# Seven block products for the first feed-forward product, and a first batch that stays in SBUF

## The chip, the cores and the metric

The program runs on one core of one Trainium2 chip. The metric is the device time of one execution in microseconds (us). The kernel before took 2764.47 us as the median of three runs (2764.15 to 2766.35). Engines are named as in the profile: PE is the matrix engine (PEld its weight loads), DVE the vector engine, ACT the scalar engine, POOL the general-purpose engine, SP the engine that issues most DMAs. The order of the instructions on each engine is fixed when the program is built.

## The reference, cut to what matters

Eight batches of 3008 tokens with 256 channels go through a Fourier mixing layer (FFT over the tokens, a complex 256x256 product, soft threshold, inverse FFT) and then through a feed-forward layer with 2048 hidden units, whose nonlinearity is h*cos(h). Behind the mixing layer `x` has shape (24064, 256), `w_in` (256, 2048) and `w_out` (2048, 256):

```python
def _moe_ref(x, w_in, w_out) -> np.ndarray:
    h = x @ w_in
    g = h * np.cos(h)
    return (g @ w_out).astype(np.float32)
```

The two weights of the feed-forward layer arrive as float64 and are decoded on the chip from their bits.

## The kernel before, in words

Three stages run for each batch `b`. Stage A (`stage_a`) multiplies the tokens by a 64-point Fourier matrix `f1`, stage B (`stage_b`) does the 47-point transforms, the complex product with the Fourier weights (`wmix`), the threshold and the first half of the inverse transform (`inverse`), in four quarters of eight frequencies each; stage C (`stage_c`) does the other half of the inverse for one tile of 512 tokens and leaves the layer's input, channels on the partitions, in SBUF. Between the stages the data goes through scratch tensors in DRAM (`scr1`, `scr2`). A batch has `NTT` = 6 tiles, the last with 448 tokens.

The feed-forward layer then runs for a tile over the `NFC` = 16 blocks of 128 hidden units, one `moe_step` each. Each operand is split into a high and a low part (type fp32r), and three products stand for one: high by high, high by low and low by high. So a step has 6 matmuls of 512 columns for `x @ w_in` (256 channels are two halves `c` of 128; lines 611 to 613) and 6 for the product with `w_out` (two halves `e` of the output channels; lines 593, 594 and 597, in `second`). Between them stand, for the step's 128x512 values in PSUM: the rounding of h/(2 pi) to an integer (ACT, line 618), the remainder (DVE, 619), the sine (ACT, 621), the product with h (DVE, 622), the high part `gh` (ACT, 623) and the low part `gl`, which takes turns between POOL (line 240, `rest_pool`) and DVE (243, `rest`). `second` runs `SKEW` = 3 steps behind, so that these six have the time of three steps; `u` has four buffers and PSUM holds three `ph`, three banks `f` for the Fourier stages, and two `po`.

The Fourier stages of the next batches are generators; `pull` takes a piece of them twice in each step, so that their matmuls stand between those of the feed-forward layer. This work is called **filler** below. Each yields its cost in PE time, and `share` spreads the sum over the tiles. A scheduler of the framework then fixes the order of the instructions on each engine.

The first batch has nobody to stand beside. Its stage A (`stage_a0`, line 299) writes to `scr1` in DRAM (line 302), its stage B loads it back (`load0`, line 360) and takes its 47-point matrices from DRAM through POOL's queue (line 386). In the same stretch the first half of the feed-forward weights is loaded and decoded in pieces of 512 elements per partition (`split_f64`, lines 201 to 212); the second half is decoded in the first tile, 0.62 pieces per step (`W_RATE`).

Of the kernel before, what the change touches and what calls it, by code (L numbers as in the profile page):

```python
# [58 lines left out]
def _constants():  # L59
# [14 lines left out]
    ei = ei.reshape(4, 32, 128).transpose(1, 0, 2).reshape(128, 128) * (2.0 / N)  # L74
# [28 lines left out]
    i1 = i1.reshape(2, 96, 96).transpose(1, 0, 2)  # L103
# [11 lines left out]
def tile_body(ctx: ExitStack, tc, x, w_r, w_i, b_r, b_i, w_in, w_out,  # L115
# [11 lines left out]
    ff = cp.tile([128, 256], F32, name="ff")  # L127
    nc.gpsimd.dma_start(ff, c_ff)
# [12 lines left out]
    def load_constants():  # L141
        with nc.allow_non_contiguous_dma(reason="bias"):
            for r, bsrc in enumerate((b_r, b_i)):
                nc.gpsimd.dma_start(bb[:, r, :], bsrc.rearrange("(c p) -> p c", p=128))
        nc.gpsimd.dma_start(sig, c_sig)
        nc.gpsimd.dma_start(fi[0], c_if)

# [11 lines left out]
    win = cp.tile([128, 2, 2, FF], F32R, name="win")  # L159
    wout = cp.tile([128, 2, NFC, 256], F32R, name="wout")  # L160
# [5 lines left out]
    fi, ws = {}, {}  # L166
# [16 lines left out]
    def load_f64(src):  # L183
        if "pro" in pool:
            raw = pool["pro"].tile([128, 1024], U32, tag="xp", name="raw", bufs=XP_BUFS)
        else:
            raw = wk.tile([128, 1024], U32, tag="raw", name="raw", bufs=1)
        with tc.issue_after(mark["b0"].ins):
            nc.gpsimd.dma_start(raw if len(src.shape) == 2 else raw.rearrange("p (f e) -> p f e", f=2), src)
        return raw  # L190

    def split_f64(hi, lo, raw):
# [3 lines left out]
        m = wk.tile([128, 512], F32, tag="yh", name="wm", bufs=2)  # L196
        a = wk.tile([128, 512], F32, tag="wa", name="wa", bufs=1)
        q = wk.tile([128, 512], F32, tag="yl", name="wq", bufs=2)
# [11 lines left out]
        nc.scalar.copy(hi, a)  # L210
        rest_pool(a, a, hi)
        ve.tensor_tensor(out=lo, in0=a, in1=q, op=ALU.add)  # L212

    pieces = []
    for q in range(4):
        for c in range(2):
            cs = slice(512 * q, 512 * q + 512)
            pieces.append((win[:, 0, c, cs], win[:, 1, c, cs], w_in[128 * c:128 * c + 128, 1024 * q:1024 * q + 1024]))
        for f in (4 * q, 4 * q + 2):
            pieces.append((wout[:, 0, f:f + 2].rearrange("p f e -> p (f e)"),  # L220
                           wout[:, 1, f:f + 2].rearrange("p f e -> p (f e)"),
                           w_out[128 * f:128 * f + 256, :].rearrange("(f p) e -> p f e", p=128)))
    raws, mark = [], {}

    def load_piece():
        k = len(raws)
        if k < len(pieces):
            raws.append(load_f64(pieces[k][2]))

    def moe_w():  # L230
        for k, (hi, lo, _) in enumerate(pieces):
            while len(raws) <= k:
                load_piece()
            split_f64(hi, lo, raws[k])
# [14 lines left out]
    def fps(name):  # L249
        if "pro" in pool:  # L250
            if not banks:
                banks.extend(("f", "h", "o0", "f", "h", "o1", "f", "h"))
            tag = banks.pop(0)
            return ps.tile([128, 512], F32, tag=tag, name=name, bufs=1 if tag[0] == "o" else 3)
        return ps.tile([128, 512], F32, tag="f", name=name, bufs=3)
# [31 lines left out]

    def stage_a0():

        scr1[0] = dr.tile([32, 96, 256], F32, tag="scr1", name="scr1_0")  # L290
        dst = scr1[0].rearrange("s (r i) d -> (s r) i d", r=4)
        xs = []
        for c in range(6):
            xs.append(pool["pro"].tile([128, 1024], F32, tag="xp", name="x0", bufs=XP_BUFS))
            nc.sync.dma_start(xs[c], x[0, :, 1024 * c:1024 * (c + 1)])
        landed("x0", xs[5][:, :1])
        for c in range(12):
            p = fps("pa")
            mm(p, ff[:, :128], xs[c // 2][:, 512 * (c % 2):512 * (c % 2) + 512], start=True, stop=True)
            ao = stage_in("ao0") if c % 2 else stage_out("ao0")  # L300
            mark["a0", c % 2] = (nc.vector.tensor_copy if c % 2 else nc.scalar.copy)(ao, p)
            mark["a0"] = nc.sync.dma_start(dst[:, 2 * c:2 * c + 2, :], ao.rearrange("p (i d) -> p i d", i=2))
            if c == 5:
                load_fourier_w()

    def stage_a(b):
# [4 lines left out]
        def load(c):  # L311
            if c < 12:
                ld[c] = stage_in("xt")
                with tc.issue_after(mark["at0", 2].ins) if b == 1 else ExitStack():
                    nc.sync.dma_start(ld[c], x[b, :, 512 * c:512 * (c + 1)])

        def prep(c):
            if b > 1 and c < 12:
                xt = ld.pop(c)
                xh = wk.tile([128, 512], F32R, tag="xh", name="xh", bufs=3)  # L320
                xl = wk.tile([128, 512], F32R, tag="xl", name="xl", bufs=3)
# [10 lines left out]
        for c in range(12):  # L332
            load(c + ahead)
            prep(c + 1)
            p = fps("pa")
            if b == 1:
                mm(p, ff[:, :128], ld.pop(c), start=True, stop=True)
# [7 lines left out]
            nc.sync.dma_start(dst[:, 2 * c:2 * c + 2, :], ao.rearrange("p (i d) -> p i d", i=2))  # L345
            yield 0.65


    def stage_b(b):
        scr2[b] = dr.tile([4, 24, 32, 256], F32, tag="scr2", name=f"scr2_{b}")  # L350
        dst = scr2[b].rearrange("r i s d -> (r i) s d")
# [4 lines left out]
        def load0(v):  # L356
            if v < 8:
                at0[v] = pool["pro"].tile([128, 1024], F32, tag="xp", name="at0", bufs=XP_BUFS)[:96]
                at0[v] = at0[v].rearrange("p (s d) -> p s d", s=4)
# [401 lines left out]
```

## Time and profile before

The table is of the profiled execution, which took 2764.63 us; 2762.9 of them lie between the first and the last instruction (the span).

| what | us |
|---|---|
| median of three runs | 2764.47 |
| profiled execution, whole | 2764.63 |
| its span | 2762.9 |
| first matmul of the feed-forward layer | 142.5 |
| first output of tile 0 copied from PSUM | 214.9 |
| last output written, issue | 2757.7 |

The last three rows are times from the span's start. A profile gives for each engine the time in which it was busy. A group of instructions shows its line in the kernel, its operation, output and inputs, the shape, the count, the busy time and the mean time of one, and the idle time ahead with what ended it. The chain of waits follows the work that ended last back to its start. There a matmul's length is the distance to the next one, while in a group its length includes the time until its result is out; only the former adds up.

### The profile page before, as it was taken

How to read it: one execution, taken by the hardware profiler on the slowest of the kernel's cores; microseconds unless marked ns; L12 is line 12 of the kernel's file. 1: busy time of each engine (PE TensorE's matmuls, PEld its weight loads, DVE VectorE, ACT ScalarE, POOL GpSimd, SP SyncE). 2: the span in 40 equal slices, each digit the busy share in tenths (PEclk: the TensorE clock that was granted, in tenths of full speed). 3: DMA queues.
4: the chain of work that ended last, by engine and by line, in shares of the span. 5: the costliest groups of instructions: out<-in, count | busy, mean ns of one | idle time of the engine just before them, and what ended most of it. 6: DMA issues, size and time to landing. Idle time of an engine off the chain costs nothing.

```text
span 2762.9 us, 37050 instructions
## 1 busy us (share of the span) xinstructions
PE 2717.8 (98%) x13286; PEld 2298.8 (83%) x13286; DVE 1851.6 (67%) x2920; ACT 1751.5 (63%) x3236; POOL 905.2 (33%) x707
## 2 busy tenths in 40 slices
PE   6899999999999999999999999999999999999999
PEld 4478888888888888888888888888888888888888
DVE  3697766767756776677766777667776677666665
ACT  2566666666666666666666666666666666666666
POOL 3364332334323442243322433233332323222222
PEclk8999999999999999999999999999999999999999
DMA  8421221122111221112211122111222111011000
GB/s 251 156 88 50 78 66 62 47 67 82 44 59 55 68 77 51 53 53 72 71 64 41 58 69 72 64 37 55 70 68 67 31 43 56 28 48 33 8 16 15
DMA packets 115753, 172.34 MB, mean 62 GB/s; under 512 B 13008, under 2 KB 64960, under 8 KB 115568
## 3 DMA queue, kind: packets, MB, share of 16 engines
q1 hardware_dynamic: 109632, 151.04, 17.4%
q0 software_dynamic: 5936, 18.92, 2.2%
q8 instruction: 105, 1.72, 0.3%
q14 instruction: 80, 0.66, 0.1%
HBM read 94.94 MB, written 74.97 MB: 61 GB/s over the span
## 4 chain that ended last, share of the span: by engine, by line
PE 95%; DVE 2%; DMA 2%; ACT 1%; issue 0%; POOL 0%; SPq 0%; ACTq 0%; POOLq 0%; DVEq 0%
PE po L593 12%; PE ph L611 12%; PE po L594 12%; PE po L597 12%; PE ph L613 12%; PE ph L612 12%; PE pb L397 3%; PE pc L574 3%; PE pi L509 3%; PE pw L443 2%; PE pw L441 2%; PE pw L442 2%; PE pt L476 2%; PE pw L437 1%; PE pa L341 1%; PE pa L340 1%
## 5 line engine op out<-in xcount | busy, mean ns | idle before, releaser
L240 POOL TENSOR_TENSOR gl<-u,gh 128x512 fp32r<-128x512 f32 (+1 forms) x384 | 492.3, 1282 | 1536.5 <-ACT gh L623 1254.3
L622 DVE TENSOR_TENSOR u<-ph,u 128x512 f32<-128x512 f32 (+1 forms) x768 | 521.2, 679 | 300.8 <-ACT u L621 287.9
L619 DVE SCALAR_TENSOR_TENSOR u<-ph,u 128x512 f32<-128x512 f32 (+1 forms) x768 | 519.7, 677 | 297.1 <-ACT u L618 295.2
L621 ACT ACTIVATE u<-u 128x512 f32<-128x512 f32 (+1 forms) x768 | 480.0, 625 | 327.8 <-DVE u L619 325.2
L618 ACT ACTIVATE u<-ph 128x512 int32<-128x512 f32 (+1 forms) x768 | 450.8, 588 | 307.2 <-PE ph L613 298.4
L611 PE MATMUL ph<-xTh,win 128*128 128x512 f32 (+1 forms) x1536 | 611.2, 398 | 2.9 <-DVE u L622 2.8
L593 PE MATMUL po<-gh,wout 128*128 128x512 f32 (+1 forms) x1536 | 601.9, 392 | 0.0
L613 PE MATMUL ph<-xTh,win 128*128 128x512 f32 (+1 forms) x1536 | 595.5, 388 | 2.5 <-DVE win L212 2.5
L623 ACT CAST gh<-u 128x512 fp32r<-128x512 f32 (+1 forms) x768 | 468.1, 609 | 204.2 <-DVE u L622 200.6
L594 PE MATMUL po<-gh,wout 128*128 128x512 f32 (+1 forms) x1536 | 595.4, 388 | 0.0
L612 PE MATMUL ph<-xTl,win 128*128 128x512 f32 (+1 forms) x1536 | 594.1, 387 | 0.0
L597 PE MATMUL po<-gl,wout 128*128 128x512 f32 (+1 forms) x1536 | 477.0, 388 | 0.5 <-POOL gl L240 0.5
L243 DVE TENSOR_TENSOR gl<-u,gh 128x512 fp32r<-128x512 f32 (+1 forms) x384 | 316.3, 824 | 79.4 <-ACT gh L623 74.1
L613 PEld LDWEIGHTS ph<-xTh,win 128*128 128x128 f32 x1536 | 288.4, 188 | 57.5 <-DVE win L212 3.0
L611 PEld LDWEIGHTS ph<-xTh,win 128*128 128x128 f32 x1536 | 289.3, 188 | 51.2 <-DVE u L622 3.9
L597 PEld LDWEIGHTS po<-gl,wout 128*128 128x128 f32 x1536 | 286.3, 188 | 54.4 <-POOL gl L240 0.7
L593 PEld LDWEIGHTS po<-gh,wout 128*128 128x128 f32 x1536 | 289.0, 188 | 50.7
L594 PEld LDWEIGHTS po<-gh,wout 128*128 128x128 f32 x1536 | 288.9, 188 | 50.9 <-DVE wout L212 0.4
L612 PEld LDWEIGHTS ph<-xTl,win 128*128 128x128 f32 x1536 | 289.3, 188 | 47.0
L397 PEld LDWEIGHTS pb<-f,at 96*128 96x128 f32 x896 | 121.1, 191 | 9.5 <-DVE Xl L402 0.5
L495 DVE SCALAR_TENSOR_TENSOR yl<-pt,sig,yh 96x256 fp32r<-96x256 f32 x224 | 103.8, 474 | 34.8 <-ACT yh L494 33.4
L240 POOL TENSOR_TENSOR xl<-xt,xh 128x512 fp32r<-128x512 f32 x72 | 99.2, 1378 | 80.1 <-PE pa L342 49.3
(109 smaller groups left out, 2769.7 us busy)
## 6 DMA issues: line engine op xcount, KB each, us to landing
scr<-ao SPq DMA_DIRECT2D x96, 256.0 KB, 2.3
scr<-bo SPq DMA_DIRECT2D x128, 192.0 KB, 2.1
bt<-scr SPq DMA_DIRECT2D x192, 128.0 KB, 2.6
xt<-in_dram SPq DMA_DIRECT2D x84, 256.0 KB, 2.9
at<-scr SPq DMA_DIRECT2D x112, 192.0 KB, 2.6
out_dram<-ob SPq DMA_DIRECT2D x80, 256.0 KB, 2.2
raw<-in_dram POOLq DMA_DIRECT2D x16, 512.0 KB, 4.7
f<-in_dram POOLq DMA_DIRECT2D x56, 144.0 KB, 3.0
```

The costliest lines, as they stand in the source:

```text
L240: return nc.gpsimd.tensor_tensor(out=lo, in0=x, in1=hi.bitcast(F32), op=ALU.subtract)
L593: mm(po[e][:, :n], wout[:, 0, f, es], gh[:, :n], start=f == 0, stop=False)
L594: mm(po[e][:, :n], wout[:, 1, f, es], gh[:, :n], start=False, stop=False)
L597: mm(po[e][:, :n], wout[:, 0, f, es], gl[:, :n], start=False, stop=f == NFC - 1)
L611: mm(h, win[:, 0, c, fs], th[:, c, :n], start=c == 0, stop=False)
L612: mm(h, win[:, 0, c, fs], tl[:, c, :n], start=False, stop=False)
L613: mm(h, win[:, 1, c, fs], th[:, c, :n], start=False, stop=c == 1)
L618: nc.scalar.activation(k[:, :n], h, AF.Identity, bias=0.25, scale=1.0 / TWO_PI)
L619: nc.vector.scalar_tensor_tensor(out=u[:, :n], in0=h, scalar=1.0 / TWO_PI, in1=k[:, :n], op0=ALU.mult, op1=ALU.subtract)
L621: nc.scalar.activation(u[:, :n], u[:, :n], AF.Sin, bias=HALF_PI, scale=TWO_PI)
L622: nc.vector.tensor_tensor(out=u[:, :n], in0=h, in1=u[:, :n], op=ALU.mult)
L623: nc.scalar.copy(gh[:, :n], u[:, :n])
```

## The change: what it does

**Seven products for eight.** Two blocks of hidden units (a pair `fp`) and the two halves of a tile (256 tokens each) are taken together. With the two channel halves this is a product of 2x2 blocks, done by Strassen's scheme in Winograd's form: seven products of 128x128 by 128x256 where there were eight. Each product still has three matmuls, now of 256 columns: 21 per pair, where two steps had 12 of 512. The last tile is also done with 512 columns in this product (before: 448).

- The block sums of the weights are made once, while the weights are decoded (`win_blocks`: four sums on POOL for each quarter of `w_in`; `win` holds seven blocks per pair). The sums of the input are made in `stage_c` for each tile: seven blocks `xh`, `xl`, through four DVE subtractions and one on POOL of 256 columns, and their high and low parts.
- The sums of the results are made in PSUM. `moe_pair` keeps two banks: `hA` with blocks c11 and c22, `hB` with c12 and c21. ACT copies the first product from `hA` to `hB` (line 680) and another to `t5` in SBUF (682); DVE adds `t5` twice (692 and 697, 256 columns each); PE goes on accumulating on what they wrote.
- The nonlinearity is done on the two banks (lines 703, 704, 714, 719 to 721, 726, 728). The low part of `hA` is now always DVE's (line 727, through 267), that of `hB` always POOL's (729, through 264). Half of this work is put off into the next pair (`tail`). `u` has two buffers (`UB`), PSUM two banks each of `hA`, `hB` and `f`.

**The first batch.** Its stage A takes `x` as the stationary operand and the Fourier matrix as the moving one (line 335): 48 matmuls of 128 columns. The result `a0`, channels on the partitions, stays in SBUF. `turn` transposes it, four blocks at a time, on PE (line 397) to what stage B needs. The write to `scr1` and the loads from it are gone for this batch, and the 47-point matrices come early, on SP's queue (`load_f0`).

**Weights.** All of `w_in` (8 pieces) is decoded ahead of the feed-forward layer, and all of `w_out`, in 16 pieces of 256 elements, in the first tile, 2.5 pieces per pair.

**Smaller edits.** `scr2` has another order of axes, so that stage C loads a half tile with one DMA of 256 KB and not two of 128. `wmix` copies two of its three products by ACT into their place, where it copied one. The sums of the two parts in stage B are made in halves of 384 elements on POOL, with one buffer. `xh`, `xl` of stage A have one buffer each.

What the scheduler makes of a pair is seen on PE in the last batch, where no filler stands between. Before, one step stands as the 6 matmuls of `second` and the 6 of the first product (the last three rows stand twice):

```order
L593 MATMUL po_23717<-gh,wout 128x512 [waits Activation_49]
L594 MATMUL po_23717<-gh,wout 128x512
L593 MATMUL po_23718<-gh,wout 128x512
L594 MATMUL po_23718<-gh,wout 128x512
L597 MATMUL po_23717<-gl,wout 128x512 [waits Pool_49]
L597 MATMUL po_23718<-gl,wout 128x512
L611 MATMUL ph<-xTh,win 128x512 [waits DVE_49]
L612 MATMUL ph<-xTl,win 128x512
L613 MATMUL ph<-xTh,win 128x512
```

Now, the same engine and batch. These rows stand behind the first two products of a pair (6 matmuls into `hA`), and ahead of the `gl` matmuls and another whole `second`, behind which come 6 more into `hB`:

```order
L648 MATMUL po_29191<-gh,wout 128x512 [waits Activation_49]
L649 MATMUL po_29191<-gh,wout 128x512
L648 MATMUL po_29192<-gh,wout 128x512
L649 MATMUL po_29192<-gh,wout 128x512
L675 MATMUL hB<-xTh,win 128x256 [waits DVE_49]
L675 MATMUL hB<-xTl,win 128x256
L675 MATMUL hB<-xTh,win 128x256
L675 MATMUL hB<-xTh,win 128x256 [waits Activation_49]
L675 MATMUL hB<-xTl,win 128x256
L675 MATMUL hB<-xTh,win 128x256
L675 MATMUL hA<-xTh,win 128x256 [waits Activation_49]
```

The first three rows into `hB` are the last product of one pair and wait for DVE's second add; the next three belong to the next pair and wait for ACT's copy of line 680. The scheduler has put the first products of a pair ahead of the last of the pair before.

ACT had three instructions per step, here two steps in the last batch:

```order
L618 ACTIVATE u<-ph 128x512 [waits PE_49,Activation_49]
L623 CAST gh<-u 128x512 [waits DVE_49]
L621 ACTIVATE u<-u 128x512 [waits DVE_49]
L618 ACTIVATE u<-ph 128x512 [waits PE_49,Pool_49]
L623 CAST gh<-u 128x512 [waits DVE_49]
```

Now it has eight per pair; the two copies are new, and the second rounding waits for POOL, which must have read the buffer of `u` that it overwrites:

```order
L680 COPY hB<-hA 128x256 [waits PE_49]
L703 ACTIVATE u<-hA 128x512 [waits DVE_49,Activation_49]
L682 COPY t_29929<-hA 128x256
L703 ACTIVATE u<-hB 128x512 [waits PE_49,Pool_49]
L714 ACTIVATE u<-u 128x512 [waits DVE_49]
L719 ACTIVATE u<-u 128x512 [waits DVE_49]
L726 CAST gh<-u 128x2x256 [waits DVE_49]
L728 CAST gh<-u 128x512 [waits DVE_49]
```

And DVE's row of one pair, which had five instructions for two steps (two remainders, two products, one low part) and has seven:

```order
L697 TENSOR_TENSOR hA<-hB,t_29929 128x256 [waits PE_49]
L704 SCALAR_TENSOR_TENSOR u<-hA,u 128x512 [waits Activation_49]
L692 TENSOR_TENSOR hB<-hB,t_29985 128x256 [waits PE_49,Activation_49]
L704 SCALAR_TENSOR_TENSOR u<-hB,u 128x512 [waits Activation_49]
L720 TENSOR_TENSOR u<-hA,u 128x512 [waits Activation_49]
L721 TENSOR_TENSOR u<-hB,u 128x512 [waits Activation_49]
L267 TENSOR_TENSOR gl<-u,gh 128x2x256 [waits Activation_49]
```

The rows show that the two adds (697 of one pair, 692 of the next) stand around the first remainder, so that each waits in line with the nonlinearity.

The diff, cut to what is spoken of:

```diff
-SKEW = 3
-EARLY_W = 8
+EARLY_W = 12
-W_RATE = 0.62
-POOL_GL = (0, 2)
+W_RATE = 2.5
+UB = 2
...
+    def win_blocks(q, w):
+        sm = pool["pro"].tile([128, 1024], F32, tag="xp", name="sm", bufs=XP_BUFS).rearrange("p (r k e) -> p r k e", r=2, k=4)
+        w0, w1 = (a.rearrange("p (r f e) -> p r f e", r=2, f=2) for a in w)
+        po = nc.gpsimd.tensor_tensor
+        po(out=sm[:, :, 0], in0=w0[:, :, 1], in1=w1[:, :, 1], op=ALU.add)
+        po(out=sm[:, :, 1], in0=sm[:, :, 0], in1=w0[:, :, 0], op=ALU.subtract)
+        po(out=sm[:, :, 2], in0=w0[:, :, 0], in1=w0[:, :, 1], op=ALU.subtract)
+        po(out=sm[:, :, 3], in0=w1[:, :, 0], in1=sm[:, :, 1], op=ALU.subtract)
+        for lo, hi, src in ((0, 1, w0[:, :, :1]), (1, 3, w1), (3, 7, sm)):
+            wh, wl = (win[:, h, 2 * q:2 * q + 2, lo:hi] for h in range(2))
+            nc.scalar.copy(wh, src)
+            rest(wl, src, wh)
...
-            mm(p, ff[:, :128], xs[c // 2][:, 512 * (c % 2):512 * (c % 2) + 512], start=True, stop=True)
-            mark["a0"] = nc.sync.dma_start(dst[:, 2 * c:2 * c + 2, :], ao.rearrange("p (i d) -> p i d", i=2))
+            for c in range(2):
+                for i in range(2):
+                    o, k = 256 * c + 128 * i, 512 * (n % 2) + 256 * i + 128 * c
+                    mm(p[:, o:o + 128], xs[n // 2][:, k:k + 128], fi[1], start=o == 0, stop=o == 384,
+                       skip_group_check=True)
...
+        def turn(u):
+            if b == 0 and u < 16:
+                p = fps("pq")
+                for j in range(2):
+                    for c in range(2):
+                        o = 256 * j + 128 * c
+                        nc.tensor.transpose(p[:96, o:o + 128], a0[0][:, c, 2 * u + j], ident)
+                at0[u] = pool["pro"].tile([128, 512], F32, tag="at0", name="at0", bufs=3)[:96]
+                (nc.vector.tensor_copy if u % 2 else nc.scalar.copy)(at0[u], p[:96])
...
-    def moe_step(b, t, f, pull):
+    def moe_pair(b, t, fp, pull):
+        xs = xT[b, t]
+        pa = ps.tile([128, 512], F32, tag="hA", name="hA", bufs=2)
+        pb = ps.tile([128, 512], F32, tag="hB", name="hB", bufs=2)
+        c11, c22, c12, c21 = pa[:, :256], pa[:, 256:], pb[:, :256], pb[:, 256:]
+        def product(dst, wb, xb, first=False, last=False):
+            for n, (h, x) in enumerate(((0, 0), (0, 1), (1, 0))):
+                mm(dst, win[:, h, fp, wb], xs[x][:, xb], start=first and n == 0, stop=last and n == 2,
+                   skip_group_check=True)
+        product(c11, 0, 0, first=True)
+        product(c22, 3, 3, last=True)
+        nc.scalar.copy(c21, c11)
+        t5 = pool["mo"].tile([128, 256], F32, tag="t5", name="t5", bufs=1)
+        nc.scalar.copy(t5, c22)
+        if tail:
+            next(tail[0])
+        old = second(*pend.pop(0)) if len(pend) > 2 else iter(())
+        next(old, None)
+        pull()
+        if tail:
+            next(tail.pop(0), None)
+        product(c11, 1, 1, last=True)
+        product(c21, 4, 5)
+        nc.vector.tensor_tensor(out=c12, in0=c21, in1=t5, op=ALU.add)
+        pull()
+        next(old, None)
+        product(c21, 5, 4, last=True)
+        product(c12, 6, 2, last=True)
+        nc.vector.tensor_tensor(out=c22, in0=c21, in1=t5, op=ALU.add)
...
+        start(pa)
+        pull()
+        if len(pend) > 1:
+            for _ in second(*pend.pop(0)):
+                pass
+        product(c21, 2, 6, last=True)
+        start(pb)
```

More of the change, by code (lines that the diff above doesn't have):

```diff
@@ L209, in split_f64 @@
         nc.gpsimd.tensor_tensor(out=q, in0=m, in1=q, op=ALU.mult)
[L210 to L222, printed above, removed]
+        return q
@@ L230, in moe_w @@
     def moe_w():
-        for k, (hi, lo, _) in enumerate(pieces):
+        for k in range(8 + NFC):
             while len(raws) <= k:
                 load_piece()
-            split_f64(hi, lo, raws[k])
+            if k < 8:
+                if k % 2 == 0:
+                    w = []
+                a = pool["pro"].tile([128, 512], F32, tag=f"wv{k % 2}", name="wv", bufs=1)
+                w.append(a)
+                r = decode(raws[k], 512, a)
+                nc.vector.tensor_tensor(out=a, in0=a, in1=r, op=ALU.add)
+                if k % 2:
+                    yield
+                    win_blocks(k // 2, w)
+            else:
+                load_piece()
+                a = stage_out("wa")[:, :256]
+                r = decode(raws[k], 256, a)
+                hi, lo = (wo[0][:, h, k - 8] for h in range(2))
+                nc.scalar.copy(hi, a)
+                rest_pool(a, a, hi)
+                nc.vector.tensor_tensor(out=lo, in0=a, in1=r, op=ALU.add)
@@ L528, in stage_b @@
             load(u)
-        for v in range(0 if b else 3):
-            load0(v)
-        if b == 0:
-            landed("b0", at0[1][:, 0, :1])
+        turn(0)
         yield 3.5
@@ L667, in tile_body @@
     pool["mo"] = ctx.enter_context(tc.tile_pool(name="mo", bufs=2, reuse_waits="tile"))
+    wo.append(pool["mo"].tile([128, 2, NFC, 256], F32R, name="wout", bufs=1))
     for _ in stage_c(0, 0):
         pass
+    for _ in range(2):
+        p = ps.tile([128, 512], F32, tag="hB", name="pz", bufs=2)
+        mm(p, f1[:, 0], wf[:, 0, 0].rearrange("p c e -> p (c e)"), start=True, stop=True)
     A_COST = 12 * 0.65 + 1.0
@@ L720, in pull @@
                         budget[0] -= c
-            for f in range(NFC):
+            for fp in range(NFC // 2):
                 if (b, t) == (0, 0):
@@ L733, in tile_body @@
             del xT[b, t]
+    for _ in tail[0]:
+        pass
     for p in pend:
-        second(*p)
+        for _ in second(*p):
+            pass
 def kernel(x, w_r, w_i, b_r, b_i, moe_w_in, moe_w_out):
```

265 lines of the change are left out of this document (147 added, 118 removed).

## The prediction, made before the changed kernel ran

> **What bounds the kernel now.** I read the page first: busy times, PE's row of the slices, and the engines of the chain of waits.
>
> ```profile
> PE 2717.8 (98%) x13286; PEld 2298.8 (83%) x13286; DVE 1851.6 (67%) x2920; ACT 1751.5 (63%) x3236; POOL 905.2 (33%) x707
> PE   6899999999999999999999999999999999999999
> PE 95%; DVE 2%; DMA 2%; ACT 1%; issue 0%; POOL 0%; SPq 0%; ACTq 0%; POOLq 0%; DVEq 0%
> ```
>
> PE makes 95% of the chain, and only the first two slices show it idle. Then the windows: one batch in the middle, and the pure feed-forward layer of the last batch, which has hardly any filler. Columns are PE, PEld, DVE, ACT and POOL busy, the granted clock, DMA.
>
> ```profile
> 1166.00:1502.00 336.00, 336.00 (x1676) 287.97 (x1675) 229.37 (x361) 216.02 (x402) 112.60 (x84) 1.00 0.19 61
> 2560.00:2740.00 180.00, 180.00 (x819) 151.51 (x818) 113.17 (x172) 120.64 (x212) 42.22 (x34) 1.00 0.03 12
> ```
>
> PE is busy all the time, DVE for 68%, ACT for 64%, POOL for 34% of a batch. So the time is PE's sum plus what is lost at the front; the others wait. What one matmul costs is read from the chain in order of time, as the distance of starts.
>
> ```profile
> 2561.42 0.45 PE po L597 x2
> ...
> 2564.14 0.45 PE po L597 x2
> ...
> 2741.13 0.40 PE po L597 x2
> ...
> 2743.56 0.41 PE po L597 x2
> ```
>
> A step of 12 matmuls takes 2.72 us with 512 columns (0.2267 each) and 2.43 with 448.
>
> **The first product.** It needs 256-column matmuls of the same type. The trace has a few, in the inverse transform, and one feed-forward matmul (128 weight columns) right behind one of them; and a stream of short matmuls with 128-column weights.
>
> ```profile
> 271.32 0.59 PE pi L509 x5
> ...
> 300.38 0.86 PE pb L397 x8
> ```
>
> ```profile
> 269.21 0.28 PE L509 MATMUL pi<-yh,i 96*96 96x256 f32 x1
> 269.33 0.40 PE L613 MATMUL ph<-xTh,win 128*128 128x512 f32 x1
> ```
>
> Five take 0.59 (0.118 each), and the one ahead of L613 0.12; L613's weights were loaded in that time. The stream of L397 stands at 0.108 each, which I read as the floor that the loads set. I take 0.119. A pair then has 21 x 0.119 = 2.50 us where it had 2.72: 0.221 less, for 40 pairs in 8 batches, 70.7 us. In the last tiles it has 2.50 where it had 2.43: 0.069 more for 64 pairs, 4.4 us. **PE's sum falls by 66 us.** At 0.118 it would be 74, at 0.120 58: each nanosecond is 8 us, since there are 8064 of these matmuls.
>
> The Trainium skill, "TensorE: Matmul & The Clock Gate", section "Back-to-back issue gap", gives N/2.4 + 2.5 ns for a warm matmul, 109 ns for 256 columns and 216 for 512. By that the fall would be an estimated 93 us. The rows are 10 ns above it at both lengths (118 and 227), so I stay with them.
>
> **Does the rest keep up? By sums, yes.** The durations are those of the pure stretch, and for the new shapes the nearest rows of the whole run.
>
> ```profile
> L622 DVE TENSOR_TENSOR u<-ph,u 128x512 f32<-128x512 f32 x57 | 39.4, 692 | 22.8 <-ACT u L621 20.2
> L619 DVE SCALAR_TENSOR_TENSOR u<-ph,u 128x512 f32<-128x512 f32 x56 | 38.8, 692 | 32.8 <-ACT u L618 32.8
> L240 POOL TENSOR_TENSOR gl<-u,gh 128x512 fp32r<-128x512 f32 x29 | 37.6, 1295 | 125.1 <-ACT gh L623 107.3 <-issue 13.4 <-PE po L597 4.4
> L621 ACT ACTIVATE u<-u 128x512 f32<-128x512 f32 x56 | 35.5, 633 | 12.9 <-DVE u L619 12.6
> L623 ACT CAST gh<-u 128x512 fp32r<-128x512 f32 x57 | 35.1, 615 | 4.0 <-DVE u L622 3.6
> L618 ACT ACTIVATE u<-ph 128x512 int32<-128x512 f32 x56 | 33.5, 599 | 33.5 <-PE ph L613 32.9
> L243 DVE TENSOR_TENSOR gl<-u,gh 128x512 fp32r<-128x512 f32 x29 | 19.9, 685 | 2.2 <-ACT gh L623 2.1
> ```
>
> ```profile
> L243 DVE TENSOR_TENSOR gl<-u,gh 128x512 fp32r<-128x512 f32 x320 | 276.7, 865 | 69.2 <-ACT gh L623 64.6
> L495 DVE SCALAR_TENSOR_TENSOR yl<-pt,sig,yh 96x256 fp32r<-96x256 f32 x224 | 103.8, 474 | 34.8 <-ACT yh L494 33.4
> L494 ACT ACTIVATE yh<-pt,sig 96x256 fp32r<-96x256 f32 x224 | 101.3, 465 | 8.1 <-DVE yl L495 3.8 <-PE pt L476 2.9
> L452 DVE TENSOR_TENSOR st<-pw,k 128x384 f32<-128x384 f32 x64 | 35.6, 556 | 37.5 <-ACT k L446 17.9 <-PE pw L443 14.7 <-PE pw L437 4.7
> L446 ACT COPY k<-pw 128x384 f32<-128x384 f32 x64 | 30.5, 477 | 18.3 <-PE pw L443 14.7 <-PE pw L437 3.0
> L422 POOL TENSOR_TENSOR t<-t,Xh 128x768 f32<-128x768 f32 x28 | 52.1, 1862 | 14.3 <-ACT Xh L420 14.3
> ```
>
> An add of 256 columns on DVE lies between 0.42 (the step from 384 to 512 columns, 0.136, taken off 0.556) and L495's 0.474; I take 0.45. ACT's copy of 256 lies between 0.36 (likewise from L446 and L618) and 0.465; I take 0.40. For a batch, DVE gets 96 adds, 43 us, and in stage C four subtractions of 256 and one low part of 512 instead of two of 512 for each tile, 6.7 more: 279 us. ACT gets 96 copies, 38 us, 10 in stage C and 4 in the complex product: 268. POOL gets some 3.3 per tile in stage C: 133. PE has 336 - 8 = 328. That is 85%, 82% and 41%: none passes PE.
>
> **By order, only just.** In a pair, DVE and ACT hand the work to each other: add (697), rounding, remainder, add (692), second remainder, second sine, second product, low part, and then the next add. The hand-overs are seen in any step:
>
> ```profile
> 999.42 0.60 ACT L618 ACTIVATE u<-ph 128x512 int32<-128x512 f32 x1 [0.76 <-PE ph L613]
> ...
> 1000.78 0.63 ACT L621 ACTIVATE u<-u 128x512 f32<-128x512 f32 x1 [0.25 <-DVE u L619]
> ```
>
> ```profile
> 1000.05 0.69 DVE L619 SCALAR_TENSOR_TENSOR u<-ph,u 128x512 f32<-128x512 f32 x1 [0.67 <-ACT u L618]
> ```
>
> 0.03 us from ACT to DVE, 0.04 back. The loop is 0.45 + 0.60 + 0.69 + 0.45 + 0.69 + 0.63 + 0.69 + 0.685 = 4.89, with four hand-overs 5.03 us, and at most 5.25 (adds of 0.474, the low part at the 0.865 that L243 has over the whole run, where POOL works beside it more). PE's pair is 2.50 + 2.72 = 5.22. So without filler PE still ends last, by 0.2 us; before, three steps (8 us) lay between the first product and its use. The new waits stand in front of much. PE's matmuls behind either add hold back the two or four products after them and `second`; the copy of line 680 holds back three products. ACT's second rounding waits for POOL's low part of the pair before, and holds back both sines, both high parts and the next copy. Its loop (rounding, remainder, sine, product, high part 0.615, POOL 1.295, hand-overs) is 4.77 us.
>
> With filler PE has more to do: a batch less its 48 pairs of the old kind (40 x 5.44 + 8 x 4.86 = 256.5) leaves 79 us, 1.64 per pair, so a pair lasts 6.86. DVE's filler is 62 us per batch (229 less 48 pairs of two remainders, two products and one low part at 0.865, plus 6.7), 1.29 per pair, ACT's 1.1 (216 less 48 times six, plus 14). Were all of DVE's and half of ACT's in the loop, it would be 5.03 + 1.29 + 0.55 = 6.87, as long as PE's 6.86. With buffers cut (two `f` banks for three, two of `u`, one `xh`), some pairs will miss. The bounds are nothing (PE was busy 336 of 336 us with the same filler) and the price of the slower rival below. I take nearer to nothing: 0.35 us, a third of one POOL sum of 384 elements (half of L422, 0.93), for each of the 28 quarters of stage B: **+10 us**.
>
> **The front.** The chain of waits, PE's rows at the end of stage A and in stage B, and two windows:
>
> ```profile
> 15.06 5.74 DMA scr<-ao
> ...
> 21.52 4.27 DMA scr<-ao
> ...
> 26.43 4.63 DMA at<-scr
> ...
> 37.73 10.46 DMA f<-in_dram
> ```
>
> ```profile
> 13.38 5.43 PE L299 MATMUL pa<-x,ff 128*128 128x512 f32 x12 [1.20 <-DMA x<-in_dram]
> 29.86 7.09 PE L410 MATMUL pb<-f,at 96*128 96x144 f32 x32 [11.05 <-DMA at<-scr]
> ...
> 48.23 2.29 PE L410 MATMUL pb<-f,at 96*128 96x144 f32 x8 [3.51 <-DMA f<-in_dram]
> ```
>
> ```profile
> 30.00:136.00 106.00, 89.42 (x346) 55.88 (x346) 61.42 (x113) 53.46 (x108) 47.02 (x51) 0.87 0.60 182
> 144.00:208.00 64.00, 57.16 (x264) 46.47 (x263) 59.95 (x81) 43.90 (x79) 39.76 (x32) 0.97 0.24 72
> ```
>
> The trip through DRAM goes; stage A ended at 18.8, so with the first transposes and their copy stage B starts near 20.5 and not at 29.86: 9.4 us less. The wait of 3.5 us for the 47-point matrix goes, and a clock of 0.87 in the mean rises to near 1 with PE no longer idle, some 4 us. Added are 64 transposes, 7 us at 0.108; the block sums on DVE, 9 us at L243's rate, on POOL and ACT, beside a PE that was busy for 89 of 106 us: 2 us shown. Stage C must finish its block sums before the first product, 2.5 us more. Sum: **-5.5 us**, between -20 (transposes and sums all hidden, the later stall of DVE gone too) and +8 (DVE's 9 us and the 7 all on the path). In tile 0, DVE is what ends last (59.95 of 64 us): 16 adds more, 7 us, and 16 short pieces instead of 8 long ones: **+8 us**, between 0 and +12. At the end the last pair's nonlinearity is one stretch, of about 1.5 us more.
>
> **Sum.** 2764.6 (the profiled execution; 0.2 above the median of the runs shown, span 2762.9) - 66.3 - 5.5 + 8 + 10 + 1.5 = **2712 us**.
>
> **Rivals.**
> - *Nothing is lost.* Filler leaves the loops time, 0.118 holds, the front gives 15: 2764.6 - 74 - 15 + 4 + 1.5 = 2681. For it: the busy shares. Against: loops of 5.03 beside 5.22.
> - *POOL in ACT's way (slower).* A quarter puts eight POOL sums of about 0.93 with ACT's copies between them into the same line as the low parts. Two of them ahead of one make the loop through ACT's second rounding 4.77 + 1.9 = 6.6, with ACT's filler 7.7, above 6.86; a quarter touches some four pairs. At 3.5 us per quarter, 98 us: 2800. It decides from 2.2 us per quarter ((66.3 + 5.5 - 8 - 1.5) / 28). For it: the three steps that a late low part had are one pair now. Against: POOL is busy for 41% only, and PE's slack is larger where the filler is long.
> - *Half matmuls for whole loads (no change).* The first product doubles the loads for a column. At 0.1255 per matmul PE's sum falls by 14 us only, which the other terms (-5.5 + 8 + 10 + 1.5 = 14) eat: 2765. By the step from 256 to 512 columns 256 columns cost 0.109, as much as the 0.108 of L397's loads, so that load and matmul could get in each other's way in a long stream. Against: the 0.12 ahead of L613.
> - The skill's same page, "The mechanism" in the part on packing, says that a load overlaps a running matmul only in another row group. By that 21 loads in the open would cost more than the change saves. The 0.2267 for 512 columns, with a load each, does not agree; I give it nothing.
>
> **Chances.** Forecast (2690 to 2745) 0.45, nothing lost 0.25, slower 0.16, no change 0.06, between 2745 and 2759 0.08. What a measurement here can tell from no change is about 0.2%, 5.5 us: faster 0.78, same 0.06, slower 0.16. The range goes from 2660 (nothing lost, with 0.117 and so 82 from PE, the front at -20, tile 0 at 0) to 2790, most of the way to the slower case.
>
> **What would show it.** Starts of L675's matmuls 0.118 to 0.120 apart; a batch of 327 to 331 us; first feed-forward matmul near 137 us. Wrong: PE waiting often for the adds of lines 692 and 697 or the copy of 680, ACT's line 703 for POOL; a distance above 0.125.

## The result and the profile after

The changed kernel took 2843.32 us (median; 2841.53 to 2847.6), the kernel before 2764.74 beside it: a ratio of 1.0286, 95% interval 1.0268 to 1.0303. It is 79 us slower; 2712 were predicted. The page of the changed kernel, its busy times and PE's slices:

```profile
PE 2729.5 (96%) x16880; PEld 2435.7 (86%) x16880; DVE 2153.0 (76%) x3892; ACT 2083.0 (73%) x4276; POOL 1137.2 (40%) x987
PE   8789999999999999999999999999999999999998
```

It looks like before: PE at 96%, everybody else far below. The windows tell more. Columns are as in the prediction; a batch in the middle, then four pairs of the last batch without filler, and the 21 us right behind them, in which stage C makes the sums for the next tile:

```profile
862.00:1205.00 343.00, 334.17 (x2105) 301.62 (x2105) 263.53 (x476) 254.85 (x527) 139.85 (x118) 1.00 0.19 59
2621.20:2642.29 21.09, 21.09 (x133) 19.03 (x132) 15.73 (x29) 16.34 (x33) 5.18 (x4) 1.00 0.00 1
2642.29:2663.37 21.08, 19.86 (x125) 17.36 (x124) 17.30 (x29) 16.07 (x33) 7.76 (x6) 1.00 0.05 18
```

The batch has 9 us in which PE does nothing, where before it had none. Pairs without filler have none now either: PE works 21.09 of 21.09 us, 5.27 per pair. It stands still where stage C's sums come. PE's busy time is modelled: a matmul that is stretched by a late successor counts as busy. The distances of starts are plainer. The median of the 8064 matmuls of line 675 is 0.120 us, as forecast, but their mean is 0.135, together 1092 us where 8064 x 0.120 = 968: **124 us more than their medians lie between them and whatever PE does next.** Some of the waits of the whole run (engine, line, what was waited for; us in total, times, longest):

```profile
DVE u L704 <- ACT u L703: 254.3, 301, 1.8
ACT u L703 <- DVE hA L697: 100.0, 90, 3.5
DVE hA L697 <- PE hB L675: 87.1, 89, 3.1
DVE hB L692 <- PE hB L675: 50.3, 89, 1.5
PEld hB L675 <- DVE hA L697: 38.2, 47, 2.0
PE hB L675 <- DVE hA L697: 26.6, 30, 1.8
ACT u L703 <- POOL gl L264: 26.6, 73, 0.9
PE po L648 <- ACT gh L728: 20.6, 38, 1.6
```

PE waits for DVE's add, DVE for PE's product, ACT for the add: a ring in which each waits for the next. Where the time went, from the copies of the last outputs of each tile out of PSUM (ACT, line 657; before, line 601), in us:

| stretch | before | after | difference |
|---|---|---|---|
| start to first feed-forward matmul | 142.5 | 127.3 | -15.2 |
| to the end of tile 0 | 73.5 | 90.3 | +16.8 |
| rest of batch 0 | 279.0 | 302.4 | +23.4 |
| six batches | 2004.2 | 2049.7 | +45.5 |
| last batch | 259.0 | 267.1 | +8.1 |

Some 14 us of batch 0's row are filler that PE now takes on earlier (57 matmuls of each kind in `wmix` instead of 39 fall into it).

### The profile page after: what moved, and what is told of

It is laid out like the page before. It is cut to its first block, busy times and chain, and to the rows that moved or that the text cites. A ratio compares the mean times of both kernels' runs of the same rounds, so it can differ in the third digit from the quotient of the medians.

```text
span 2842.1 us, 46744 instructions
## 1 busy us (share of the span) xinstructions
PE 2729.5 (96%) x16880; PEld 2435.7 (86%) x16880; DVE 2153.0 (76%) x3892; ACT 2083.0 (73%) x4276; POOL 1137.2 (40%) x987
## 5 line engine op out<-in xcount | busy, mean ns | idle before, releaser
L264 POOL TENSOR_TENSOR gl<-u,gh 128x512 fp32r<-128x512 f32 x384 | 518.0, 1349 | 1187.0 <-ACT gh L728 806.5
L675 PE MATMUL hB<-xTh,win 128*128 128x256 f32 x3072 | 740.4, 289 | 27.9 <-DVE hA L697 26.6
L675 PEld LDWEIGHTS hB<-xTh,win 128*128 128x128 f32 x3072 | 549.7, 190 | 67.9 <-DVE hA L697 38.2
L675 PE MATMUL hA<-xTh,win 128*128 128x256 f32 x2304 | 549.5, 288 | 9.6 <-DVE u L720 6.5
L704 DVE SCALAR_TENSOR_TENSOR u<-hA,u 128x512 f32<-128x512 f32 x384 | 264.6, 689 | 243.0 <-ACT u L703 241.5
L675 PE MATMUL hB<-xTl,win 128*128 128x256 f32 x1536 | 434.7, 283 | 0.0
L675 PEld LDWEIGHTS hA<-xTh,win 128*128 128x128 f32 x2304 | 412.6, 191 | 23.1 <-issue 4.8
L267 DVE TENSOR_TENSOR gl<-u,gh 128x512 fp32r<-128x512 f32 x384 | 300.2, 782 | 38.6 <-ACT gh L726 35.6
L675 PE MATMUL hA<-xTl,win 128*128 128x256 f32 x1152 | 327.0, 284 | 1.1 <-POOL xTl L264 0.6
L675 PEld LDWEIGHTS hB<-xTl,win 128*128 128x128 f32 x1536 | 292.7, 191 | 23.8
```

The source lines that it names most:

```text
L264: return nc.gpsimd.tensor_tensor(out=lo, in0=x, in1=hi.bitcast(F32), op=ALU.subtract)
L267: return nc.vector.tensor_tensor(out=lo, in0=x, in1=hi.bitcast(F32), op=ALU.subtract)
L675: mm(dst, win[:, h, fp, wb], xs[x][:, xb], start=first and n == 0, stop=last and n == 2, skip_group_check=True)
L704: nc.vector.scalar_tensor_tensor(out=u, in0=p, scalar=1.0 / TWO_PI, in1=u.bitcast(I32), op0=ALU.mult, op1=ALU.subtract)
```

## The experiments

All times are medians beside runs of the kernel before on the same chip (2763.5 to 2764.8). "Batch" is the mean length of batches 1 to 5, "last" that of the last batch, both from the copies of the outputs as above.

| kernel | us | ratio to before, 95% | batch | last |
|---|---|---|---|---|
| before | 2764.7 | | 335.4 | 259.0 |
| changed | 2843.3 | 1.0268-1.0303 | 343.3 | 267.1 |
| plain | 2757.1 | 0.9965-0.9984 | 335.4 | 259.0 |
| no_adds | 2716.5 | 0.9815-0.9844 | 325.7 | 253.5 |
| adds_aside | 2807.0 | 1.0135-1.0169 | 335.2 | 291.1 |
| adds_short | 2820.4 | 1.0186-1.0217 | 342.1 | 265.7 |
| c_nolow | 2788.8 | 1.0072-1.0106 | 338.8 | 260.1 |
| c_nolow_ub3 | 2817.9 | 1.0179-1.0210 | 341.6 | 259.4 |
| c_dve | 2859.1 | 1.0329-1.0360 | 344.8 | 265.9 |
| gl_pool | 2831.0 | 1.0231-1.0261 | 339.8 | 273.7 |
| spread | 2847.1 | 1.0283-1.0314 | 344.4 | 267.3 |
| spread_glpool | 2838.1 | 1.0251-1.0285 | 340.0 | 273.7 |
| prio | 2830.0 | 1.0220-1.0250 | 340.1 | 267.3 |
| prio_glpool | 2883.6 | 1.0415-1.0449 | 348.5 | 285.8 |
| short_second | 2695.6 | 0.9736-0.9765 | 326.6 | 252.8 |
| pad | 2887.9 | 1.0433-1.0464 | 349.6 | 275.7 |

**Three theories at the start.** In the last batch most pairs last 5.27 us, but 5.86, 7.34 and 6.79 about once a tile, around stage C's sums. There DVE's subtractions of two SBUF tiles are long exactly while POOL has one. DVE, POOL and ACT of the changed kernel, in order of time (start, length):

```profile
2654.42 0.42 DVE L697 TENSOR_TENSOR hA<-hB,t 128x256 f32<-128x256 f32 x1
2654.76 1.71 DVE L267 TENSOR_TENSOR xTl<-ta,xTh 128x512 fp32r<-128x512 f32 x1
2656.39 1.77 DVE L267 TENSOR_TENSOR gl<-u,gh 128x512 fp32r<-128x512 f32 x1
```

```profile
2654.63 1.28 POOL L264 TENSOR_TENSOR xTl<-ta,xTh 128x512 fp32r<-128x512 f32 x1 [0.73 <-ACT xTh L633]
2655.87 1.75 POOL L264 TENSOR_TENSOR gl<-u,gh 128x512 fp32r<-128x512 f32 x1
```

```profile
2658.20 0.60 ACT L703 ACTIVATE u<-hA 128x512 int32<-128x512 f32 x1 [2.03 <-DVE gl L267]
```

ACT's rounding stands idle for 2.03 us behind the 1.77, since it overwrites the buffer of `u` that this low part reads. So theory 1 was this collision; theory 2, the amount of work put into a loop without slack; theory 3, too few buffers. By matmul distances above their medians, the pairs with stage C's work and the ones right behind them, some 160 of 376, lost 90 us outside tile 0; the same measure over all of PE's matmuls gives 124 there.

**c_dve: stage C's POOL work to DVE.**

```diff
-                rest_pool(xl[:, :2], xb, xh[:, :2])
+                rest(xl[:, :2], xb, xh[:, :2])
...
-            nc.gpsimd.tensor_tensor(out=tb[:, 1], in0=b1[:, 1], in1=tb[:, 0], op=ALU.subtract)
+            ve(out=tb[:, 1], in0=b1[:, 1], in1=tb[:, 0], op=ALU.subtract)
...
-                (rest if k == 3 else rest_pool)(xl[:, k:k + 2], tt, xh[:, k:k + 2])
+                rest(xl[:, k:k + 2], tt, xh[:, k:k + 2])
```

> In stage C the three POOL instructions of a tile (the low parts of lines 617 and the second of 633/634, the sum of line 628) are done by DVE. Theory 1 (DVE's SBUF subtractions are stretched from 0.7 to 1.7 us while POOL works on SBUF, and the pairs around stage C, which lose some 90 us in all, lose them by that): DVE's own subtractions in these pairs return to 0.7 us and the time falls by 30 to 80 us, to 2765-2815. Theory 2 (it is the amount of work that stage C puts into a loop without slack, whoever stands beside it): DVE has 0.69 + 0.42 + 0.69 = 1.8 us more per tile, and the time rises by up to 48 x 1.8 = 86 us, to 2850-2930. Theory 3 (too few buffers for u, f, gh): within 10 us of 2843.

16 us slower. DVE's low parts by shape, of the changed kernel and then of this one (count, busy us, mean ns):

```profile
L267 DVE TENSOR_TENSOR xTl<-ta,xTh 128x512 fp32r<-128x512 f32 x48 | 53.3, 1110 | 2.3 <-ACT xTh L633 2.1
```

```profile
L267 DVE TENSOR_TENSOR xTl<-ta,xTh 128x512 fp32r<-128x512 f32 x96 | 73.7, 801 | 0.6 <-ACT xTh L633 0.5
L267 DVE TENSOR_TENSOR xTl<-xb,xTh 128x512 fp32r<-128x512 f32 x48 | 33.6, 701 | 15.4 <-ACT xTh L615 15.4
```

The collision is mostly gone from stage C (0.80 and 0.70 for 1.11 us) and the kernel is slower, where theory 1 expected it to be faster. The work costs its place in DVE's line, though less than the most that theory 2 allowed. The run does not part the two: what the collision cost and the 1.8 us of new work on DVE per tile stand in one sum. A bound for the collisions is what they lengthen on DVE: 48 x (1.110 - 0.685) for stage C and 384 x (0.782 - 0.685) for `gl`, 57 us in the whole changed kernel, and no run shows how much of that PE waits for.

**c_nolow: stage C without low parts.** Lines 616, 630 and 634 are taken out and `xl` is one tile of zeros.

> Leaves out the low parts of the feed-forward layer's input: stage C makes no low part (lines 617, 630, 634) and the products take zeros in their place; all matmuls stay. It prices these low parts, 0.45 + 0.68 us on DVE and 1.3 + 1.6 us on POOL per tile. Theories 1 and 2: most of the 90 us lost in the pairs around stage C goes, 2765-2790. Theory 3 (buffers): little changes, 2825-2843.

55 us faster, 1.1 us for each of 48 tiles. That is as much as these instructions take on DVE, which the page shows busy for only 76%. The run takes their work and their collisions away together, so that it does not part theories 1 and 2 either.

**gl_pool: both low parts of `gl` on POOL.**

```diff
-            rest(la, ua, ga)
+            rest_pool(la, ua, ga)
```

> Both low parts of gl on POOL (line 727 as line 729). DVE loses 0.69 us per pair, POOL gets 1.3 more (2.6 of 5.3). Theory 1 and 2 alike: DVE's loop falls from 5.0 to 4.4 us and leaves 0.6 us of slack per pair, so that a fall of 30 to 90 us, to 2750-2815, would show DVE's line as the cause. Theory 3: POOL frees the buffers of u 1.3 us later, ACT's line 703 waits longer for POOL, and the time rises, to 2880-2990.

Only 12 us faster, short of the range. Batches gain 3.5 us each, the last loses 6.6 (pairs of 5.33 to 5.35 us there, 5.6 in the last tile). ACT's line 703 now waits 69.3 us for POOL and not 26.6, and 43.2 for DVE's add and not 100.0: one wait is traded for another, with a small gain.

**plain: eight plain products, the rest of the change kept.** Step, stage C, banks and `win` are those of before; front, decoding in pieces, `scr2` and small edits those of the change.

> The changed kernel with eight plain products (512 columns, the step, stage C and three banks of before), so only the first batch, the weight pieces and the small edits are left of the change. If the front alone does what the traces show (first feed-forward matmul 15 us earlier, tile 0 about 10 us longer because all of w_out is decoded there): 2750-2762, and a batch of 335.4 us as before. If the small edits (buffers of stage A and B, scr2's order) cost something in every batch: 2765-2800, with batches longer than 335.4.

```profile
822.00:1157.50 335.50, 335.50 (x1673) 287.54 (x1672) 218.41 (x360) 221.21 (x413) 114.58 (x100) 1.00 0.19 60
```

PE is busy 335.50 of 335.50 us, as before the change. The rest of the change is a gain of 7.2 us in all (2764.4 was measured beside it), and the seven products cost 86 (2843.3 - 2757.1). This version does the whole work and beats both kernels, the one before by 0.3%.

**spread: stage C in five pieces.** The cost that stage C announces to `share` rises with it, from 5.22 to 7.86 us.

```diff
             ve(out=tb[:, 0], in0=b22, in1=ta[:, 0], op=ALU.subtract)
+            ve(out=x2l, in0=b22, in1=x2h.bitcast(F32), op=ALU.subtract)
+            yield 0.7
             nc.gpsimd.tensor_tensor(out=tb[:, 1], in0=b1[:, 1], in1=tb[:, 0], op=ALU.subtract)
             ve(out=ta[:, 1], in0=tb[:, 0], in1=b1[:, 0], op=ALU.subtract)
-            ve(out=x2l, in0=b22, in1=x2h.bitcast(F32), op=ALU.subtract)
+            yield 0.7
...
                 (rest if k == 3 else rest_pool)(xl[:, k:k + 2], tt, xh[:, k:k + 2])
+                yield 0.7
```

> Stage C's second half comes in five pieces over about two pairs and not in one (PSUM is read first, then sums, then the high and low parts); no instruction is added or removed. If the loss is that the 3 us of DVE and 3 of ACT fall into one pair with about 2 us of slack (lumps): some 30 to 50 of the 90 us go, 2795-2815. If a pair's loop is full wherever the work is put (amount): within 10 us of 2843.

**spread_glpool: the same, with gl_pool's edit.**

> The spread stage C, and both low parts of gl on POOL, which alone took 12 us off. Lumps: the two add up, or more, since DVE's loop has 0.7 us more slack in each pair: 2775-2800. Amount on DVE: 2820-2831, as with POOL alone. Amount on ACT (whose line neither edit relieves): 2820-2840.

Neither helps (2847; 2838 beside gl_pool's 2831). So it is not enough that the work comes in smaller lumps over two pairs.

**c_nolow_ub3: a third buffer of `u`** (`UB = 3`) in c_nolow, whose low parts leave room for it.

> Leaves out the same low parts of stage C's input as before (zeros in their place), and uses the room for a third buffer of u. Against 2788.75 with two buffers. Theory 3 (the second rounding, line 703, waits for POOL's and DVE's reading of u): the 50 us that PE still loses in pairs fall by half or more, 2745-2770. Otherwise the third buffer changes nothing, 2783-2793.

29 us slower than with two buffers, which no theory expected; 13 of them in batch 0. The order on all engines changed with the buffer: on DVE, 41% of the instructions have the same place in both runs. Theory 3 gets no support, but with the order changed it is not refuted either; the cause of the rise was not pursued.

**no_adds, adds_aside, adds_short: the four instructions that Strassen's scheme adds to a pair.** no_adds takes out lines 680, 682, 692 and 697. adds_aside takes them out there and puts as many behind the first rounding:

```diff
         start(pa)
+        aside = pool["mo"].tile([128, 256], F32, tag="t5", name="t5", bufs=1)
+        for _ in range(2):
+            nc.scalar.copy(aside, c22)
+            nc.vector.tensor_tensor(out=aside, in0=c11, in1=aside, op=ALU.add)
```

> Leaves out the copies of lines 680 and 682 and the adds of 692 and 697: all seven products, each with its 21 matmuls, but their results are not summed across the banks. ACT loses 0.74 us per pair, DVE 0.85, and PE no longer waits for either between products. If the sum of matmuls was right and the loop through DVE and ACT is the whole loss: the fall forecast appears, 66 less 19 (the 512-column matmuls stand 0.231 apart and not 0.227) off the 2757 of the plain products: 2700-2720. If the loss lies in the matmuls or in stage C's buffers: 2790-2840.

> The four instructions of each pair are kept on ACT and DVE (two copies and two adds of 256 columns), but they work on the finished bank hA and write to SBUF: no matmul waits for them, and the products are not summed across the banks. It splits the 127 us between the changed kernel (2843) and the one without these instructions (2716). If it is the engines' time (0.74 us on ACT and 0.85 on DVE per pair, in full lines): 2800-2843. If it is that PE stands still while a product's sum goes through another engine's line: 2716-2750.

adds_short keeps the four in place with `[:, :32]` on each operand.

> The two copies and two adds stay where they are, and PE waits for each as before, but they do 32 columns of the 256 (the rest of the sums is left out). Engines' time: with most of 1.6 us per pair gone, 2716-2760. PE's wait for its turn in the other engines' lines, which a shorter add does not shorten: 2790-2835.

A batch of no_adds, adds_aside and adds_short:

```profile
1156.80:1483.80 327.00, 327.00 (x2106) 300.23 (x2105) 237.30 (x379) 229.66 (x432) 138.33 (x119) 1.00 0.20 62
```

```profile
1182.90:1518.30 335.40, 330.95 (x2105) 301.06 (x2103) 272.93 (x475) 253.92 (x527) 139.65 (x118) 0.99 0.19 61
```

```profile
1197.70:1539.90 342.20, 334.32 (x2105) 302.23 (x2104) 241.53 (x474) 237.66 (x528) 141.06 (x118) 1.00 0.19 59
```

Without the four, PE is busy 327.00 of 327.00 us with all its matmuls: the gain forecast on PE is there, and these instructions eat it. They cost 127 us in all (2843.3 - 2716.5), and they cost it around stage C: the last batch, with stage C of four tiles and no other filler, is 13.6 us longer with them, a full batch, with six tiles and all the rest, 17.6. That is about 3 us for a tile in both, so that stages A and B seem to add little. Their time alone costs half of that in a batch (335.2 between 325.7 and 343.3). Their place alone, at 32 columns, costs nearly all (342.1); but a copy or an add of 32 columns still takes 0.18 to 0.20 us, half of the time of 256, so time and waiting are not cleanly parted. The parts add up to more than the whole (90 + 104 for 127 us), as they would where either of two delays is enough; that reading is not tested, and the order differs from run to run. adds_aside's last batch of 291 us, 38 of its 90, is a case of its own: the scheduler put the two low parts of a pair next to each other, and DVE's took 1.00 to 1.78 us beside POOL's.

**prio: the four ahead of all else that is ready.**

```diff
+        with tc.high_priority():
             nc.vector.tensor_tensor(out=c12, in0=c21, in1=t5, op=ALU.add)
```

and likewise around the other three.

> The two copies and two adds are given to the scheduler with the highest priority, so that they go ahead of whatever else is ready on ACT and DVE; nothing else is edited. If the loss is made by the order on these engines (an add that stands behind a product, a low part or a filler that PE does not need yet): a fall of 20 to 80 us, 2760-2820. If the order does not matter: within 10 us of 2843. If the remainder and the sine that are pushed back are as urgent: slower, 2850-2880.

13 us faster, between the ranges for an order that matters and one that does not. This order is better; whether another one would win more is not shown.

**short_second and pad: PE's own work made less and more.** The first cuts lines 649 and 653 to `[:, :64]`, the second adds two matmuls to a pair.

> In the second product the matmuls with the low part of the weights and with gl do 64 columns of the 512 (the rest of these two products is left out): PE has some 1.6 us less per pair, 0.03 for 0.23 at eight matmuls, while ACT, DVE and POOL keep all they do. A pair's length is now that of the loop through ACT and DVE. If PE's sum is the bound of the changed kernel, with stalls on top: the time falls by most of 384 x 1.6 = 610 us, below 2400. If the loop is nearly as long as PE's pair, as its 5.03 us beside 5.27 say, and filler lengthens both alike: a fall of only 40 to 150 us, 2690-2800, and pairs without filler of about 5.0 us.

> Two matmuls of 256 columns more in each pair (two products add their last term twice), 0.24 us of PE or 91 us in all; nothing else. If PE is the bound and its stalls stand where they are: 2843 + 91 = 2934. If pairs with stalls are as long as the loop, the added work fills part of the 120 us that PE waits: a rise of 40 to 70 us only, 2880-2915.

The expectation mis-sized PE's relief: a matmul of 64 columns starts 0.03 us ahead of its successor, but the one of 512 ahead of it then takes 0.31 and not 0.23. By median distances PE has 0.92 us less per pair, 352 in all, and the time falls by 148. DVE's line of two pairs without filler, from the product of line 720 on:

```profile
2444.32 0.68 DVE L720 TENSOR_TENSOR u<-hA,u 128x512 f32<-128x512 f32 x1
2444.92 0.68 DVE L721 TENSOR_TENSOR u<-hB,u 128x512 f32<-128x512 f32 x1
2445.52 0.42 DVE L697 TENSOR_TENSOR hA<-hB,t 128x256 f32<-128x256 f32 x1
2445.85 0.68 DVE L267 TENSOR_TENSOR gl<-u,gh 128x512 fp32r<-128x512 f32 x1
2447.38 0.69 DVE L704 SCALAR_TENSOR_TENSOR u<-hA,u 128x512 f32<-128x512 f32 x1 [0.85 <-ACT u L703]
2448.34 0.69 DVE L704 SCALAR_TENSOR_TENSOR u<-hB,u 128x512 f32<-128x512 f32 x1 [0.26 <-ACT u L703]
2448.95 0.42 DVE L692 TENSOR_TENSOR hB<-hB,t 128x256 f32<-128x256 f32 x1
2449.28 0.68 DVE L720 TENSOR_TENSOR u<-hA,u 128x512 f32<-128x512 f32 x1
2449.87 0.68 DVE L721 TENSOR_TENSOR u<-hB,u 128x512 f32<-128x512 f32 x1
2450.47 0.42 DVE L697 TENSOR_TENSOR hA<-hB,t 128x256 f32<-128x256 f32 x1
...
2455.43 0.42 DVE L697 TENSOR_TENSOR hA<-hB,t 128x256 f32<-128x256 f32 x1
```

The loop lasts 4.95 us from one add of line 697 to the next, with PE's pair at about 4.35. What closes it stands on ACT and POOL:

```profile
2445.04 0.62 ACT L726 CAST gh<-u 128x512 fp32r<-128x512 f32 x1 [0.30 <-DVE u L720]
2445.63 0.62 ACT L728 CAST gh<-u 128x512 fp32r<-128x512 f32 x1
...
2447.71 0.60 ACT L703 ACTIVATE u<-hB 128x512 int32<-128x512 f32 x1 [0.36 <-POOL gl L264]
```

```profile
2446.38 1.29 POOL L264 TENSOR_TENSOR gl<-u,gh 128x512 fp32r<-128x512 f32 x1 [3.67 <-ACT gh L728]
```

From the product of line 720 (2444.32) through both high parts, POOL's low part, the second rounding, the second remainder and the add of 692 to the next 720 (2449.28) are 4.96 us. So this is the loop through POOL, in an order that is not quite the changed kernel's (there 692 stands ahead of the second remainder). In a batch with filler:

```profile
1154.70:1479.50 324.80, 301.55 (x2105) 278.20 (x2104) 259.15 (x475) 252.84 (x527) 139.80 (x118) 0.98 0.20 63
```

324.80 us (326.6 in the mean of five), where the changed kernel's PE has 328.2 by its median distances. PE can still hold the ring up here, so that the ring alone is at most that. **With filler the ring is about as long as PE's work; without, PE's pair is longer, 5.27 beside 4.95.** pad agrees: its pairs without filler last 5.51, all of the 0.24 us more, and of the 91 us added to PE in all 44.5 are seen, so that the rest fell into time in which PE waited.

**prio_glpool: both edits that had helped.**

> The two edits that took 13 and 12 us off are put together: the copies and adds first among what is ready, and both low parts of gl on POOL. If order and room in DVE's line are two causes: 2815-2822. If they are one, whichever edit gives it: 2825-2832. The eight plain products with the new front took 2757, so that neither would beat them.

53 us slower than either. Its pairs without filler last 5.83 us, where prio's last 5.27 and gl_pool's 5.33; each edit gained in the order that it was tried in, and together they make a third order.

## Why the prediction was wrong, step by step

**The step that failed** is the price at the end of "By order, only just": +10 us for pairs that miss, 0.35 for each of stage B's 28 quarters. In its place the runs show about 127 us (the changed kernel less no_adds), and at another spot: some 3 us for each tile's stage C, whether stages A and B stand beside it or not. Stage C's new work had entered the loop only as a mean over 48 pairs (6.7 us of DVE in a filler of 62 per batch). Of the 131 us between 2712 and 2843 this term is about 117, PE's old matmuls are 16 and tile 0 is 9, while the front gave back 10 (below). The waits named as a sign of being wrong are the ones seen: PE for DVE's add, ACT for POOL.

What led to the small price was right in part. Without filler PE does end last, by 0.3 us. With filler the prediction found the loop as long as PE's pair, 6.87 beside 6.86; the runs have 324.8 / 48 = 6.77 and 328.2 / 48 = 6.84. That its 5.03 is so near to the 4.95 measured is luck: the 5.03 ran through both of DVE's adds and DVE's low part, the 4.95 runs through POOL's low part, for which the prediction had 4.77. And from two chains of one length it went on to a loss near nothing.

Why stage C's pairs lose so much is open. Three things come together there: DVE and ACT get more work in a pair, POOL's subtractions stretch DVE's, and the rounding waits for a buffer of `u`. One explanation is that equal means do not make equal pairs, and that a pair takes the longer of the two. A calculation was made from the traces of the six batches between the first and the last: PE's medians sum to 1948 us, the lengths of short_second's pairs to 1944, the longer of the two pair by pair to 2154, of two pairs taken together to 2068, and the changed kernel took 2048. It comes near the sum with a freely chosen slack, but it does not find the pairs: what it adds to a single pair and what PE loses there have a correlation of 0.04. spread, which was to make the pairs more even, did not help either. So this is not shown. What the runs do show: less work for DVE, or for ACT and DVE, makes the kernel faster (no_adds, c_nolow, gl_pool), more on DVE makes it slower (c_dve), and less work on PE brings 148 of 352 us.

**PE's sum** was right as to the new matmuls: 0.119 to 0.120, and four of the five batches of no_adds last 327.0 to 327.2, at the lower end of the forecast 327 to 331. It was mis-sized as to the old ones. In the changed kernel those of 512 columns stand 0.231 apart, not 0.227 (median of 3840; plain still has 0.227), and the pair takes 5.27, not 5.22; 16 us over 320 pairs.

```profile
2684.83 0.40 PE L648 MATMUL po<-gh,wout 128*128 128x512 f32 x1
2685.06 0.40 PE L649 MATMUL po<-gh,wout 128*128 128x512 f32 x1
2685.30 0.39 PE L648 MATMUL po<-gh,wout 128*128 128x512 f32 x1
2685.53 0.40 PE L649 MATMUL po<-gh,wout 128*128 128x512 f32 x1
2685.76 0.28 PE L675 MATMUL hB<-xTh,win 128*128 128x256 f32 x1
```

The four stand 0.23, 0.24, 0.23 and 0.23 apart, 0.93 for the 0.91 of before.

**The front** was better than forecast: the first feed-forward matmul at 127.3, not 137. Stage B began where it should (transposes at 20.64, its first matmul at 21.97, forecast 20.5), so the trip through DRAM is gone as forecast. The 7 us of transposes and 2 of block sums that the prediction set on the path, and 2.5 for stage C's, were too much: plain, which has the transposes and no block sums, starts at 125.3, so that all block sums together cost 2. How much of the transposes was hidden is not shown. The clock term fits: PE was granted 1.00 from 30 to 120 us, and 0.87 before (30 to 136).

```profile
20.64 1.49 PE L397 MATMUL pq<-ident,a 128*96 128x128 f32 x12 [1.62 <-DVE a L337]
21.97 1.21 PE L450 MATMUL pb<-f,at 96*128 96x144 f32 x8
```

**Tile 0** cost 16.8, not 8, and outside its range of 0 to 12. In the plain kernel it costs 5 (125.3 to 204.0 against 142.5 to 216.0), so that is the decoding. The other 11 are open. DVE is busy for 83.8 of 90.3 us there (76.8 of 78.7 in plain), and no_adds, with the four instructions gone, takes only 2 us less, so that they are not the main part of it. PE's granted clock was 0.82 there, 0.93 in plain and 0.98 before; what that cost is not parted.

**Rivals.** The slower one ended nearest, 2800, but with another place: it put POOL's sums of stage B in ACT's way. Line 703 waited 26.6 us for POOL and 100.0 for DVE's add, and gl_pool, with twice the low parts on POOL, is faster. It was right in this, that the loop through POOL's low part is the one that closes when PE is relieved (short_second). "Half matmuls for whole loads" is ruled out by the 0.120. The rule that the prediction weighed last, of the Trainium skill's "TensorE: Matmul & The Clock Gate", "The mechanism", that a load overlaps a running matmul only in another row group, does not agree with it either: with 21 loads in the open the matmuls could not stand 0.120 apart.

## What to carry to other kernels

When a change takes work from the busiest engine and gives a little to the others, add up the ring through which they wait for each other, at its place and with its filler, not each engine's share: here, with PE at 96%, DVE at 76% and ACT at 73%, four instructions of 0.4 us per pair on ACT and DVE cost 127 us, while 352 us less of PE brought 148. If the ring and the busiest engine come out within a few per cent, do not price the loss near nothing: look for the stretch where the ring gets the most work, price it there, and test it by leaving that work out. And where a scheduler makes the order, a small edit is also a new order: measure edits together before adding up their gains.

## What the runs showed of the hardware

A DVE subtraction of two SBUF tiles takes 0.68 us where it starts ahead of POOL's (the row at 2445.85 above) and 1.7 behind the start of a POOL subtraction (the rows at 2654.76): it ends 0.56 us behind the end of POOL's, at 2655.91, and POOL's next, 1.75 long and not 1.28, waited in its turn. The Trainium skill, "SBUF — State Buffer", section "SBUF: two separate sides", calls the port that the two share an exclusive lock, held for a whole instruction. By that the second of two waits for all of the first, and these rows agree. On PE, matmuls of 512 and 64 columns in turn start 0.31 and 0.03 us after one another (medians in short_second), where those of 512 alone stand 0.23 apart: the cut to 64 columns saves 0.12 us and not 0.20. That it is the weight load of the short one's successor that is paid there is a reading that no run tests.
